# Low words on other engines, and a planner's constants chosen anew

## The chip, the core and the metric

The kernel runs on one core of one Trainium2 chip. A core has TensorE (matrix products, in the profile PE, with its weight loads as PEld), VectorE (DVE), ScalarE (ACT), GpSimd (POOL) and SyncE (SP), which here only issues transfers. Each engine works off its own instructions in order; semaphores tie the engines together. SBUF is the working memory, PSUM takes TensorE's results in banks. The metric is the time of one execution in device microseconds, the median of several runs.

## The reference

Causal attention by blocks of 64, then a feed-forward network over all 4608 tokens, in fp32:

```python
scores = scale * np.matmul(q, k.transpose(0, 1, 3, 2))          # 8 batches, 8 heads, 576 x 576, head size 64
scores = np.where(pos[:, None] // 64 >= pos[None, :] // 64, scores, -1e9)
attn = np.exp(scores - scores.max(-1, keepdims=True))
attn = attn / (attn.sum(-1, keepdims=True) + 1e-9)
x = np.matmul(attn, v).transpose(0, 2, 1, 3).reshape(4608, 512)
h = x @ w_in                                                    # 512 x 2048
out = (np.maximum(h, 0) + alpha * np.minimum(h, 0)) @ w_out     # 2048 x 512
```

The two weight matrices arrive as float64 and reach the chip as pairs of 32-bit words, a low and a high one.

## The kernel before

**Attention** goes over 32 pairs of heads (`NPAIR`), four per batch. For a pair, `scores` runs three groups of query blocks (`TOP`, `MID`, `LOW`): small tiled products on TensorE (L721), maxima per row on VectorE (L726), four exchanges of 32 partitions on GpSimd (`swap`, L698), a minimum on VectorE (L729), exponentials on ScalarE (L734) and transposes on VectorE (L738). `factors_of` makes the reciprocal row sums, `values` the tiled products with v (L780) and the scaling on VectorE (L786). The first 256 rows of a batch run one batch ahead of the others (`SKEW`); so the four pairs of batch 0 come first, with `E0` and `E1` in their priorities.

**The network** is done in two halves. The first six of 16 blocks of the hidden width (`FA`) are worked off during attention, chunk by chunk of 256 tokens: `split_x` parts x in a high and a low piece, `ffn1` makes the hidden products (L508), `activate` the leaky step (L519, L521) and the split of its result into gh (L525 or L527) and gl on GpSimd (L530), `ffn2` the second product (L547). The sum of this half goes to memory (`part`). The other ten blocks come after attention: `later_weights` prepares them, two at a time, `factors` prepares x in 512 tokens, `pair1` makes seven products instead of eight (L588) with additions on VectorE (L597, L601), and `ffn2` and `store_out` finish (L547, L876). Every fp32 product is three products of rounded pieces: high by high, high by low, low by high.

**Conversion of weights** (`to_f32`) makes fp32 out of the word pairs for 128 x 512 values: a load into `raw` (SP), the exponent on VectorE (L391) and ScalarE (L394), the high mantissa on VectorE (L396) and ScalarE (L402), the sign (L399, VectorE), then mantissa = low word x 2^-52 + high part (L403, VectorE), and the product of both parts on GpSimd (L406). There are 32 of them: 12 early ones for the first half (`first_weights`, priorities `C0 + C1 * (f + i / 2)`), 16 during attention whose results are put into memory (`weights_ahead`, priority `5 * p + 100`), and four in `later` for the first pair of blocks: two of w_in at priority `SOON`, two of w_out after attention. Buffers of `raw` and `m` are handed out in program order (`IN_ORDER`). `split` then rounds a weight to its high piece on ScalarE (L411) and subtracts for its low piece (L412), in the second half on the engine that `LATER` names.

**The order** of all this is not written by hand. `Plan.op` collects every step with its engine, an estimated cost, what it reads and writes, and a priority (low goes first); `schedule` plays the engines through in time, and always lets the ready step of lowest priority go whose buffers are free. The resulting order is issued as the program. So a constant that changes no instruction can still change the order on every engine. Attention of pair p has priorities about `5 * p`, with offsets for maxima (`PM`), exponentials (`PX`), transposes (`PT`), row sums (`PZ`) and scaling (`PU`), and `VL` for the load of v; FFN products get theirs from `turn`, and what empties their banks has `FP`. `SHIFTS` adds an amount to all steps of a given priority. `NEAR` lets TensorE stay with tiled products when one is ready whose priority is at most that much higher; `c_tiled` charges `SWITCH` for them, and `schedule` takes it off again when two tiled ones follow one another. `RB`, `EB` and `EF` are the numbers of buffers for `raw`, `m` (converted words) and `ef`.

Of the kernel before, what the change touches and what calls it, by code (L numbers as in the profile page):

```python
# [32 lines left out]
FIRST, THEN = (3, 2, 1, 0), (4,)  # L33
SKEW = 1
DUOS, HB, AB, HT, AM, AT, WB = 3, 2, 1, 3, 2, 4, 4
C0, C1 = -6, 4.5
WARM, WARM_END = 10, 3400
TICK, FULL_COLUMNS, SP0 = 3413.33, 3060, 700
LAG = 5.5
VL = 1.0  # L40
E0, E1 = -2, 1.5
NEAR = 8
FP = -1
AHEAD = {(8, 0): 5, (8, 1): 6, (9, 0): 7, (9, 1): 8, (10, 0): 10, (10, 1): 11, (11, 0): 12, (11, 1): 14, (12, 0): 15, (12, 1): 16, (13, 0): 18, (13, 1): 19, (14, 0): 20, (14, 1): 21, (15, 0): 23, (15, 1): 24}
SHIFTS = {}
SOON, XB = 220, 1004.7
FEW = 10
BEGIN = {"SP": SP0, "ACTQ": SP0, "POOLQ": SP0, "PE": WARM_END, "ACT": 2000, "DVE": 1500, "POOL": 1700}
B1 = 20
RB, EB, EF = 2, 3, 6  # L50
LO_A = ("POOL", "POOL")
QA, VA = 3, 1
PB, QB, VB, TB, CB = 5, 3, 3, 2, 6
SWAP = ("POOL", "POOL", "POOL", "POOL")
RCP = ("ACT", "ACT", "ACT", "ACT")
PM, PX, PT, PZ, PU = -8, -4, -1, -1, -2
XO, XF = 2, 1
GH, XH, XC = ("ACT", "ACT", "POOL"), "ACT", 2
LATER = ("POOL", "POOL", "POOL", "POOL", "POOL", "POOL")
GB = 6  # L60
LAT = {"PE": 240, "DVE": 140, "ACT": 137, "POOL": 95}
LONGER = 1.06
# [23 lines left out]
class Plan:  # L86
# [16 lines left out]
    def op(self, engine, cost, fn, r=(), w=(), prio=0.0, claim=(), then=None, ends=()):  # L103

        i = len(self.ops)
        prio += SHIFTS.get(round(prio, 4), 0.0)
        deps = {j for j, o in enumerate(self.ops) if any(b.kind in ends for b in o[4])} if ends else set()
        for k in r:
            if k in self.writer:
                deps.add(self.writer[k])  # L110
        for k in w:
            if k in self.writer:
                deps.add(self.writer[k])
            deps.update(self.readers.get(k, ()))
        for k in r:
            self.readers.setdefault(k, []).append(i)
        for k in w:
            self.writer[k] = i
            self.readers[k] = []
        bufs = dict.fromkeys(k[0] if isinstance(k, tuple) else k for k in (*r, *w, *claim))  # L120
        bufs = [b for b in bufs if isinstance(b, Buf)]
        for b in bufs:
            b.users += 1
            if b.users == 1 and b.kind in IN_ORDER:
                b.after = self.last.get(b.kind)
                self.last[b.kind] = b
        deps.discard(i)
        self.ops.append((engine, cost, fn, deps, bufs, prio, then))
        return i
# [147 lines left out]
    return (93 if sbuf else 51) + n / 1.2  # L277


SWITCH = 420  # L280


def c_pool(n):
# [18 lines left out]

def c_tiled(n, count):

    return Products(max(4 * n / 2.4, 11 * count) + SWITCH, max(4 * n / 1.2, 22 * count) + 2 * SWITCH, 4 * n, True)


@with_exitstack
def attn_ffn(ctx, tc, qT, kT, vT, w_in, w_out, alpha, out):
# [63 lines left out]
    def to_f32(src, prio, after=(), early=None):  # L373
# [12 lines left out]
        def fr():  # L386
# [13 lines left out]
            out=e(), in0=high(), scalar=-2 ** 31, in1=e(), op0=ALU.bitwise_and, op1=ALU.bitwise_or),  # L400
            r=[raw], w=[ea], prio=prio)
        op("ACT", c_act(512, True), lambda: nc.scalar.activation(out=eb(), in_=fr(), func=AF.Copy, scale=2.0 ** -20), w=[eb], prio=prio)  # L402
        op("DVE", Beside(600), lambda: nc.vector.scalar_tensor_tensor(  # L403
            out=mb(), in0=low(), scalar=2.0 ** -52, in1=eb(), op0=ALU.mult, op1=ALU.add),
            r=[raw, eb], w=[mb], prio=prio)
        op("POOL", c_pool(512), lambda: nc.gpsimd.tensor_tensor(out=mb(), in0=mb(), in1=e().bitcast(F32), op=ALU.mult), r=[ea], w=[mb], prio=prio)  # L406
        return mb, mb

# [454 lines left out]

    def second_room():
        rooms("fx", ("w1", 2, [2, 7 * 256], F32R), ("w2", 4, [2, 512], F32R), ("X", 6, [2, 512], F32R),
              ("g", 2, [CHA], F32), ("gh", 2, [CHA], F32R), ("gl", 2, [CHA], F32R))
    op("NONE", 0, end_first, r=[("xd", b, i, pair) for b in range(B) for i in range(2) for pair in range(NP)], ends=("wa", "xh", "xl", "xc", "xo"), prio=0, then=second_room)

    def store_out(acc, t):
# [55 lines left out]
```

## Time and profile before

| | us |
|---|---|
| Median of the runs (3) | 1053.79, from 1052.94 to 1057.25 |
| Profiled execution, its own time | 1054.86 |
| Its span, first to last instruction | 1053.0 |
| TensorE busy | 1002.1 (95%) |
| VectorE, ScalarE, GpSimd busy | 731.2, 594.0, 586.0 |
| Attention's last tiled product ends | 514.0 |
| First product of the second FFN half starts | 570.2 |

A row of busy time by stage has from:to, its length, then for TensorE, its weight loads, VectorE, ScalarE and GpSimd the busy us and in brackets the instructions, then the granted TensorE clock (1 is full), the busy share of the DMA engines, and GB/s. A row of waits says which engine and line was idle for whom: total us, times, longest. A group of instructions has line, engine, operation, output<-inputs and shapes, count, then busy us, mean ns of one, and the idle time before them. A row in order of time begins with start and length.

### The profile page before, as it was taken

The page shows a single profiled execution, that of the slowest core. Times are in us where ns is not written, and L with a number is a line of the kernel's source. Part 1 is how long each engine was busy: PE and PEld are TensorE (multiplying, and loading weights), DVE is VectorE, ACT ScalarE, POOL GpSimd, SP SyncE. Part 2 cuts the span into 40 slices and gives each one's busy share as a digit, 9 for nine tenths or more (in the row PEclk, how much of TensorE's full clock was granted, in tenths as well). Part 3 has the DMA queues.
Part 4 walks back from the last instruction along what each step waited for, and adds up shares of the span by engine and source line. Part 5 has one row for each costly group of instructions (what it writes and reads, how often), then busy time and mean ns, then how long its engine had stood idle before and what let it go on. Part 6 is the DMA issues. An engine that isn't in the chain of part 4 may idle for free.

```text
span 1053.0 us, 32747 instructions
## 1 busy us (share of the span) xinstructions
PE 1002.1 (95%) x12860; PEld 876.3 (83%) x12860; DVE 731.2 (69%) x1654; ACT 594.0 (56%) x2124; POOL 586.0 (56%) x1038
## 2 busy tenths in 40 slices
PE   5477999999999999999999999999999999999998
PEld 4365788888888888888888988989898989898987
DVE  6999899998786888885553675656565656565552
ACT  6967778877585777666555643434343434343431
POOL 5777647575474665656699962535353525252521
PEclk7698999999999999999999999999999999999999
DMA  8565766665756556632424222121212121212021
GB/s 280 165 218 167 221 210 221 199 213 173 225 165 224 194 166 205 204 119 81 154 71 127 75 71 81 41 80 42 81 41 81 41 81 40 82 41 81 2 81 40
DMA packets 78987, 133.73 MB, mean 127 GB/s; under 512 B 11632, under 2 KB 40048, under 8 KB 78832
## 3 DMA queue, kind: packets, MB, share of 16 engines
q1 hardware_dynamic: 78400, 131.36, 38.4%
q8 instruction: 101, 1.65, 0.7%
q14 instruction: 54, 0.44, 0.1%
q10 hardware_dynamic: 432, 0.27, 0.1%
HBM read 99.10 MB, written 32.51 MB: 125 GB/s over the span
## 4 chain that ended last, share of the span: by engine, by line
PE 65%; POOL 3%; ACT 1%; issue 1%; DVE 1%; DVEq 0%; POOLq 0%; ACTq 0%
PE bank L547 30%; PE bank L588 21%; PE bank L508 8%; PE duo L780 3%; PE duo L721 3%; POOL gl L530 1%; POOL X L412 1%; ACT p L734 1%; POOL xl L496 1%; POOL w L412 0%; POOL c L698 0%; DVE c L726 0%; DVE g L521 0%; DVE m L403 0%; POOL gh L525 0%
## 5 line engine op out<-in xcount | busy, mean ns | idle before, releaser
L530 POOL TENSOR_TENSOR gl<-g,gh 128x256 fp32r<-128x256 f32 x288 | 224.1, 782 | 281.3 <-ACT gh L527 251.7
L588 PEld LDWEIGHTS bank<-X,w 128*128 128x128 f32 x1890 | 254.4, 189 | 21.0 <-POOL X L412 1.3
L588 PE MATMUL bank<-X,w 128*128 128x256 f32 x1890 | 260.3, 282 | 1.6 <-POOL w L412 0.9
L734 ACT ACTIVATE p<-duo,c 128x256 f32<-128x256 f32 (+8 forms) x576 | 220.7, 407 | 44.0 <-DVE c L729 29.4
L547 PE MATMUL bank<-w,gh 128*128 128x512 f32 x720 | 225.4, 394 | 0.0
L519 ACT ACTIVATE g<-bank 128x256 f32<-128x256 f32 x288 | 109.1, 386 | 139.5 <-DVE bank L601 86.6
L521 DVE SCALAR_TENSOR_TENSOR g<-g,oal,bank 128x256 f32<-128x256 f32 x288 | 134.1, 473 | 66.8 <-ACT g L519 62.1
L527 ACT CAST gh<-g 128x256 fp32r<-128x256 f32 x252 | 102.4, 408 | 121.2 <-PE bank L547 93.0
L601 DVE TENSOR_TENSOR bank<-bank,g 128x256 f32<-128x256 f32 x180 | 75.4, 428 | 119.4 <-PE bank L588 116.9
L698 POOL TENSOR_SCALAR c<-c 32x4 f32<-32x4 f32 (+3 forms) x400 | 101.8, 254 | 83.1 <-DVE c L726 45.4
L547 PE MATMUL bank<-w,gl 128*128 128x512 f32 x360 | 141.9, 394 | 0.2 <-POOL gl L530 0.2
L547 PE MATMUL bank<-wa,gh 128*128 128x512 f32 x432 | 138.9, 402 | 2.5 <-ACT wa L411 1.2
L547 PEld LDWEIGHTS bank<-w,gh 128*128 128x128 f32 x720 | 121.1, 188 | 13.5
L726 DVE TENSOR_REDUCE c<-duo 128x2 f32<-128x512 f32 (+8 forms) x288 | 122.3, 477 | 13.9 <-PE duo L721 13.5
L508 PE MATMUL bank<-xh,wa 128*128 128x256 f32 x864 | 126.8, 288 | 1.7 <-POOL wa L412 1.5
L734 ACT ACTIVATION_READ_ACCUMULATOR p<-duo,c 128x1 f32 x576 | 126.0, 219 | 0.0
L508 PEld LDWEIGHTS bank<-xh,wa 128*128 128x128 f32 x864 | 113.1, 191 | 11.6 <-issue 5.4
L738 DVE STREAM_TRANSPOSE PTH<-p 128x576 f32<-128x576 f32 (+4 forms) x160 | 98.1, 627 | 8.8 <-ACT p L734 7.9
L721 PE MATMUL duo<-k,q 64*32 64x192 f32 (+4 forms) x2560 | 84.5, 373 | 19.5 <-ACT p L734 10.5
L547 PEld LDWEIGHTS bank<-wa,gh 128*128 128x128 f32 x432 | 77.9, 188 | 22.7 <-issue 3.0
L547 PE MATMUL bank<-wa,gl 128*128 128x512 f32 x216 | 85.5, 396 | 0.6 <-POOL gl L530 0.6
L597 DVE TENSOR_TENSOR g<-bank,g 128x256 f32<-128x256 f32 x135 | 56.1, 420 | 40.9 <-PE bank L588 40.7
(63 smaller groups left out, 1321.3 us busy)
## 6 DMA issues: line engine op xcount, KB each, us to landing
v<-in_v SPq DMA_DIRECT2D x32, 576.0 KB, 4.4
k<-in_k SPq DMA_DIRECT2D x32, 288.0 KB, 5.1
xb<-xd SPq DMA_DIRECT2D x9, 1024.0 KB, 5.4
m<-part SPq DMA_DIRECT2D x36, 256.0 KB, 3.2
out<-m SPq DMA_DIRECT2D x35, 256.0 KB, 2.0
va<-in_v SPq DMA_DIRECT2D x32, 256.0 KB, 3.2
raw<-in_w_in SPq DMA_DIRECT2D x16, 512.0 KB, 5.1
raw<-in_w_out SPq DMA_DIRECT2D x16, 512.0 KB, 4.6
```

The lines of the kernel that those rows point to most:

```text
L508: nc.tensor.matmul(hp()[:, :n], ww()[:, 0, cc * P:(cc + 1) * P], x()[:, cc, :n], start=(i == 0 and cc == 0), stop=(i == 2 and cc == NCC - 1))
L519: op("ACT", c_act(CHA), lambda: nc.scalar.activation(out=g(), in_=hp()[:, ts], func=AF.Relu, scale=-1.0), r=[hp], w=[g], prio=FP)
L521: op("DVE", c_dve(CHA) + 60, lambda: nc.vector.scalar_tensor_tensor(out=g(), in0=g(), scalar=oal[:, f:f + 1], in1=hp()[:, ts], op0=ALU.mul ...
L527: op("ACT", c_act(CHA, True), lambda: nc.scalar.copy(out=gh(), in_=g()), r=[g], w=[gh], prio=FP)
L530: op("POOL", c_pool(CHA) + 60, lambda: nc.gpsimd.tensor_tensor(out=gl(), in0=g(), in1=gh().bitcast(F32), op=ALU.subtract), r=[g, gh], w=[g ...
L547: nc.tensor.matmul(acc(), a()[:, ts], ww(), start=(first and i == 0), stop=(last and i == 2))
L588: nc.tensor.matmul(bank()[:, :CHA], W()[:, i, 256 * at + P * c:256 * at + P * c + P], B()[:, j, CHA * c:CHA * c + CHA], start=(n == 0), st ...
L698: nc.gpsimd.tensor_scalar(out=o, in0=i, scalar1=scale, scalar2=None, op0=ALU.mult)
L721: nc.tensor.matmul(sb()[32 * i:32 * i + 32, h, off[T]:off[T] + w], q()[hs, qs], blocks(k()[hs], T + 1, 32 * (i % 2)), start=True, stop=True)
L726: op("DVE", c_dve(2 * w), lambda t=t, w=w, o=o: nc.vector.tensor_reduce(out=c()[:, 0, 2 * t:2 * t + 2], in_=sb()[:, :, o:o + w], axis=AX.X ...
L734: op("ACT", 237 + w / 1.2, lambda x=2 * t + h, T=T, h=h, w=w, o=o: nc.scalar.activation(out=pb()[:, 2 * o + h * w:2 * o + h * w + w], in_= ...
L738: op("DVE", 85 + 2.08 * w, lambda to=to, a=a, w=w, o=o: nc.vector.transpose(out=to()[:, a:a + 2 * w], in_=pb()[:, 2 * o:2 * o + 2 * w]), r ...
```

## The change

Three edits to instructions:

- In `to_f32`, a conversion whose priority is under `LOW_POOL` = 6 no longer makes its mantissa in one VectorE instruction. ScalarE scales the low word into `m`, and GpSimd adds the high part to it.
- All six entries of `LATER` are VectorE instead of GpSimd.
- `raw` has four buffers for two, `m` four for three; in the last room gh and gl get one more buffer each instead of two.

The rest changes the planner alone: `VL`, `NEAR`, `FP`, `PM`, `PZ`, `SOON`, `XB`, the charges for tiled products, and 34 entries in `SHIFTS`, which was empty.

```diff
+LOW_POOL = 6
-VL = 1.0
+VL = 0
-NEAR = 8
-FP = -1
+NEAR = 12
+FP = 2
-SHIFTS = {}
-SOON, XB = 220, 1004.7
+SHIFTS = {38.0: 3, 36.5: 1, 28.9815: -1, 57.0: 20, 32.3148: 0.5, 169.7222: -3, 181.5741: -0.5, 148.5: -20, 168.2407: 10, 33.0: -1, -9.0: 1, 43.7963: -3, 44.537: 10, 47.0: -10, 105.0: 10, 57.1296: -3, 130.0: 3, 43.0: 20, 215.0: -1, 170.463: -20, 175.2778: -0.5, 50.463: -2, 171.9444: 20, 62.0: 10, 159.3519: -20, 133.0: 5, 154.1667: -3, 18.5: -20, 54.9074: -2, 11.5: 0.5, 36.0: 2, 43.4259: 3, 20.0: 0.5, 71.5741: 3}
+SOON, XB = 100, 1006.7
-RB, EB, EF = 2, 3, 6
+RB, EB, EF = 4, 4, 6
-PM, PX, PT, PZ, PU = -8, -4, -1, -1, -2
+PM, PX, PT, PZ, PU = -7, -4, -1, 0, -2
-LATER = ("POOL", "POOL", "POOL", "POOL", "POOL", "POOL")
+LATER = ("DVE", "DVE", "DVE", "DVE", "DVE", "DVE")
...
-SWITCH = 420
+SWITCH, RUN = 400, 160
...
-    return Products(max(4 * n / 2.4, 11 * count) + SWITCH, max(4 * n / 1.2, 22 * count) + 2 * SWITCH, 4 * n, True)
+    return Products(max(4 * n / 2.4, 11 * count) + SWITCH + RUN, max(4 * n / 1.2, 22 * count) + 2 * (SWITCH + RUN), 4 * n, True)
...
-        op("DVE", Beside(600), lambda: nc.vector.scalar_tensor_tensor(
-            out=mb(), in0=low(), scalar=2.0 ** -52, in1=eb(), op0=ALU.mult, op1=ALU.add),
-            r=[raw, eb], w=[mb], prio=prio)
+        if prio < LOW_POOL:
+            op("ACT", c_act(512, True), lambda: nc.scalar.activation(out=mb(), in_=low(), func=AF.Copy, scale=2.0 ** -52), r=[raw], w=[mb], prio=prio)
+            op("POOL", c_pool(512), lambda: nc.gpsimd.tensor_tensor(out=mb(), in0=mb(), in1=eb(), op=ALU.add), r=[eb], w=[mb], prio=prio)
+        else:
+            op("DVE", Beside(600), lambda: nc.vector.scalar_tensor_tensor(
+                out=mb(), in0=low(), scalar=2.0 ** -52, in1=eb(), op0=ALU.mult, op1=ALU.add),
+                r=[raw, eb], w=[mb], prio=prio)
...
-              ("g", 2, [CHA], F32), ("gh", 2, [CHA], F32R), ("gl", 2, [CHA], F32R))
+              ("g", 2, [CHA], F32), ("gh", 1, [CHA], F32R), ("gl", 1, [CHA], F32R))
```

## The prediction

> **What bounds the kernel now.** I read the page's head first, then the busy time by stage, then the waits of the first 120 us, and then single rows.
>
> ```profile
> span 1053.0 us, 32747 instructions
> PE 1002.1 (95%) x12860; PEld 876.3 (83%) x12860; DVE 731.2 (69%) x1654; ACT 594.0 (56%) x2124; POOL 586.0 (56%) x1038
> ...
> PEclk7698999999999999999999999999999999999999
> ```
>
> TensorE is busy for 1002.1 of 1053.0 us, and no edit takes a product away. So the time can only come out of the 50.9 us in which TensorE is idle, and out of the low clock of the first slices. The same by stage (columns: the five engines, granted clock, DMA share, GB/s):
>
> ```profile
> 0.00:10.00 10.00, 6.20 (x202) 5.04 (x202) 3.08 (x14) 2.80 (x10) 2.02 (x12) 1.00 0.80 236
> 10.00:60.00 50.00, 27.62 (x772) 20.57 (x772) 45.88 (x127) 42.85 (x195) 37.70 (x82) 0.69 0.66 222
> 60.00:120.00 60.00, 47.31 (x1088) 37.22 (x1089) 54.73 (x131) 44.47 (x182) 41.76 (x84) 0.89 0.63 196
> 120.00:500.00 380.00, 374.07 (x7258) 323.93 (x7260) 316.64 (x743) 277.25 (x1168) 230.47 (x545) 1.00 0.58 186
> 500.00:620.00 120.00, 117.37 (x894) 104.25 (x884) 64.86 (x117) 65.44 (x165) 107.65 (x128) 1.00 0.34 107
> 620.00:1000.00 380.00, 380.00 (x2381) 342.29 (x2380) 223.87 (x477) 148.23 (x375) 154.60 (x174) 1.00 0.17 57
> 1000.00:1053.00 53.00, 49.52 (x283) 43.03 (x281) 22.12 (x49) 12.92 (x34) 11.81 (x16) 1.00 0.17 60
> ```
>
> Idle time of TensorE by stage is length less busy: 3.8 us before 10, 22.4 in 10 to 60, 12.7 in 60 to 120, 5.9 in 120 to 500, 2.6 in 500 to 620, none to 1000, and 3.5 at the tail. So 35.1 of the 50.9 us lie between 10 and 120, where VectorE is busy 92% and 91%, ScalarE 86% and 74%, GpSimd 75% and 70%. The waits of the first 120 us (total, times, longest):
>
> ```profile
> POOL c L698 <- DVE c L726: 14.9, 11, 6.8
> ...
> PE duo L780 <- ACT p L734: 10.9, 5, 5.3
> PE duo L721 <- ACT p L734: 10.8, 8, 3.4
> ACT p L734 <- DVE c L729: 10.3, 5, 6.0
> ...
> POOL m L406 <- DVE m L403: 5.1, 4, 1.8
> ...
> PE bank L508 <- POOL wa L412: 1.5, 2, 1.1
> PE duo L721 <- DMA qa<-in_k: 1.5, 2, 1.3
> ...
> PE bank L547 <- ACT wa L411: 1.2, 1, 1.2
> ...
> PE bank L547 <- POOL wa L412: 1.0, 1, 1.0
> ```
>
> TensorE waits 21.7 us for exponentials; those wait for the maxima (VectorE) and their exchange (GpSimd). Another 3.7 us is for converted weights. The first FFN product starts late:
>
> ```profile
> 57.90 1.22 PE L508 MATMUL bank<-xh,wa 128*128 128x256 f32 x8
> ```
>
> Until then there is only attention to run, so every wait of its chain is idle time.
>
> **Part (a): early lows.** Conversions have priorities -6, -3.75, and so on in steps of 2.25; six of the twelve early ones lie under 6. Later ones start at 100. The prices, from the first 120 us (count, busy us, mean ns):
>
> ```profile
> L412 POOL TENSOR_TENSOR wa<-m,wa 128x512 fp32r<-128x512 f32 x12 | 15.7, 1312 | 4.4 <-ACT wa L411 4.0
> L406 POOL TENSOR_TENSOR m<-m,ef 128x512 f32<-128x512 f32 x12 | 15.3, 1274 | 5.7 <-DVE m L403 5.1
> ...
> L403 DVE SCALAR_TENSOR_TENSOR m<-raw,ef 128x512 f32<-128x512 uint32 x12 | 8.3, 695 | 0.2 <-ACT ef L402 0.2
> ...
> L402 ACT ACTIVATE ef<-ef 128x512 f32<-128x512 int32 x12 | 7.6, 633 | 1.5 <-DVE ef L396 1.4
> ```
>
> VectorE loses 6 x 0.695 = 4.2 us. ScalarE gains a scaled copy of 512 integers, like L402: 6 x 0.633 = 3.8 us. GpSimd gains an add of two 512 wide tiles, like L406: 6 x 1.274 = 7.6 us. All six lie in 10 to 60 us before, as L403's starts in the first 60 us show:
>
> ```profile
> L403 DVE SCALAR_TENSOR_TENSOR m<-raw,ef x6: 674/685/693, 15.9 to 56.3; 128x512 f32<-128x512 uint32 x6
> ```
>
> So that stage would hold 41.7 us on VectorE, 46.7 on ScalarE and 45.3 on GpSimd, of 50. The fullest engine goes from 45.9 to 46.7 us: by load alone nothing is won. What speaks for a gain is the order of the chain: it stands 25.2 us behind VectorE's reductions and minima (14.9 + 10.3). Bounds: -4.2 us, if all that VectorE sheds reaches TensorE, and +3.8 us, if all that ScalarE takes on delays exponentials. Both bounds are near; I take **-1 us**, on VectorE's side because the named waits are there.
>
> **Part (b): rings, and constants of the start.** Raw words get four buffers for two, converted words four for three; FP, PM, PZ, VL and 34 shifts reorder what is ready together. None adds an instruction. The rings allow the last six conversions, which stay on VectorE, to be loaded and begun earlier. What is there to win is the 3.7 us of waits for weights, and at most all 35.1 us of idle; to lose, two more raw loads ahead of q, k and v on SP's queue: 512 KB each at the 222 GB/s of that stage is 2.3 us, so +4.6 us, against 1.5 us of such waits now. FP = 2 lets the first two pairs go ahead of the first chunk's split; behind them wait only FFN products that cannot start before 57.9. I take **-3 us**, four fifths of the waits for weights, and nothing of the attention chain, for which no edit names a shorter path.
>
> **Part (c): tiled runs.** The charges (SWITCH 400 plus RUN 160, for 420) and NEAR 12 for 8 alter no instruction; they make the planner put tiled products (scores, values) together. Of such runs there are 55, counted in the order of time; the first and the last:
>
> ```profile
> 4.74 2.57 PE L721 MATMUL duo<-qa 64*32 64x128 f32 x128 [1.34 <-DMA qa<-in_k]
> ...
> 511.51 0.40 PE L547 MATMUL bank<-wa,gl 128*128 128x512 f32 x1
> 511.84 2.18 PE L780 MATMUL duo<-PTH,v 64*64 64x160 f32 x72
> 513.95 0.74 PE L547 MATMUL bank<-wa,gh 128*128 128x512 f32 x2
> 514.52 0.40 PE L547 MATMUL bank<-wa,gl 128*128 128x512 f32 x1
> 514.76 0.62 PE L547 MATMUL bank<-wa,gh 128*128 128x512 f32 x2
> ```
>
> Each row gives start, length and count. In this stream a 512 wide product starts 0.24 us after the one before (514.52 to 514.76). From 511.51 into the run it is 0.33, and the two behind the run take 0.57 instead of 0.48 (513.95 to 514.52). So entering and leaving cost some 0.09 us each. Five to ten runs fewer give 0.9 to 1.8 us, as many more lose that; by the wider NEAR I take **-0.5 us**, three runs fewer.
>
> **Part (d): later lows on VectorE, SOON, gh and gl, XB.** The lows and their nearest rows on VectorE, over the whole span:
>
> ```profile
> L412 POOL TENSOR_TENSOR w<-m,w 128x512 fp32r<-128x512 f32 x20 | 26.3, 1319 | 0.1
> L412 DVE TENSOR_TENSOR X<-xt,X 128x512 fp32r<-128x512 f32 x18 | 26.2, 1456 | 9.7 <-ACT X L411 9.7
> ...
> L412 POOL TENSOR_TENSOR w<-ws,w 128x512 fp32r<-128x512 f32 (+1 forms) x10 | 10.1, 1013 | 0.0
> ...
> L412 DVE TENSOR_TENSOR X<-xb,X 128x512 fp32r<-128x512 f32 x9 | 6.7, 744 | 0.0
> ```
>
> GpSimd sheds 36.4 us. VectorE takes 25 subtractions of 512 and 5 of 256 (counted as halves: 27.5) at 0.744 to 1.456 us, so 20.5 to 40.0 us. Nearly all falls into 500 to 620: GpSimd goes from 107.7 to 71 us, VectorE from 64.9 to 85 or 105 of 120. SOON lets two conversions of w_in go earlier within attention (two raw loads, eight VectorE, four ScalarE and two GpSimd instructions up to the product). Since raw buffers are handed out in program order they stay behind the 16 conversions ahead of them; running products cover them (374.1 of 380 us), and uncovered they would be four VectorE steps each, 2 x 4 x 0.695 = 5.6 us. TensorE's waits in 120 to 620:
>
> ```profile
> PE bank L588 <- POOL w L412: 0.9, 1, 0.9
> PE bank L547 <- POOL gl L530: 0.7, 2, 0.6
> PE bank L588 <- POOL X L412: 0.7, 2, 0.4
> ```
>
> That is all there is to win, 2.3 us; the products of the first FFN half cover the rest, and if that cover were gone, the uncovered excess would be what VectorE takes, 20.5 to 40 us. I take **-0.8 us**, a third, because VectorE now holds lows before the additions that free the banks. One buffer less of gh and gl costs nothing: from 620 to 1000 TensorE has no idle to show that it runs short; the same rows cover XB.
>
> The Trainium skill, SBUF — State Buffer, section "SBUF: two separate sides", says that a VectorE instruction with two SBUF inputs and a GpSimd instruction that reads SBUF exclude each other for a whole instruction. The 1456 beside the 744 ns agrees with it. By this rule alone each later low is priced at its blocked mean, 40 us, and (d) is a loss, the fourth rival below.
>
> **Part (e): the clock.** In 60 to 120 the granted clock is 0.89. If low means half, 60 x 0.11 x 2 = 13 us ran at half rate; at the busy share of 79% that lost 5.2 us. If 3 of the 12.7 us of idle go, I count that share of it: **-1.2 us** (bounds 0 and -5.2).
>
> **Sum.** -1 - 3 - 0.5 - 0.8 - 1.2 = -6.5 us. The profiled execution took 1054.86 us, 1.86 around its span, so it would become 1048.4. It is 1.07 above the median of the runs shown, 1053.79; against that median the forecast is 1047.3 us.
>
> **Rivals.**
>
> *Nothing to measure.* The load row of (a), 46.7 for 45.9 us, holds; the start stays bound by three full engines, idle merely changes place, and (c) to (e) give 1 us. Time 1052.8. For it: TensorE is at 99% from 120 us on whatever is reordered. Against it: 35.1 us of idle lie together in the stage that most constants touch.
>
> *Large gain.* The first chunk's x is done earlier, so the FFN fills the chain's waits before 57.9. Half of the 22.4 us goes, with (b) to (e): 1053.8 - 11.2 - 5.5 = 1037.1. For it: the first weights are split long before 57.9:
>
> ```profile
> 19.33 1.27 POOL L412 TENSOR_TENSOR wa<-m,wa 128x512 fp32r<-128x512 f32 x1
> ```
>
> Against it: the constants that set this pace (E0, E1, C0, C1, LAG) stay.
>
> *Slower: ScalarE and GpSimd become the early bound.* In each of six conversions a 0.63 us copy stands ahead of exponentials and a second 1.27 us add ahead of the four small exchanges that the next minimum waits for: 6 x 1.907 - 4.2 = +7.2 us, and what (b) gives is lost behind it: 1061. It decides when the idle of 10 to 60 passes 26 us and the first FFN product starts after 60. For it: both engines at over 90% of that stage. Against it: GpSimd idles 5.1 us there for L403 itself.
>
> *The later lows lock out GpSimd.* At the blocked price of 1.456 us VectorE holds 105 of 120 us in 500 to 620, each low stands ahead of the additions that free banks, and GpSimd's gl waits behind it. If the first FFN half is used up by then, the 19.5 us between the two prices reach TensorE: 1053.8 + 19.5 - 5.7 for (a), (b), (c) and (e) = 1067.6. It decides when L588 or L547 wait more than 5 us there. For it: the two prices of one instruction. Against it: VectorE is empty for 55 of these 120 us.
>
> **How the numbers follow.** A change within 0.5% (5.3 us) counts as no change. Forecast 0.45, large gain 0.08, nothing to measure 0.35, early bound 0.08, lock 0.04. Faster is 0.45 + 0.08 = 0.53, same 0.35, slower 0.12. The likeliest case by itself spans 1043 to 1049; the range 1040 to 1057 takes in the no-change case and leaves out most of the large gain and the slower ones.
>
> **What would show it.** (a) L403 runs 26 times, not 32, and VectorE's busy time in 10 to 60 falls towards 42 us while ScalarE's rises over 45. (b) TensorE's waits for wa in the first 120 us fall under 1 us, and idle in 10 to 120 is near 31. (c) Fewer than 50 tiled runs. (d) GpSimd under 80 us in 500 to 620, and no new wait of L588 or L547 for VectorE. (e) Clock over 0.91 in 60 to 120. The forecast is wrong if the idle of 10 to 120 stays over 34 us, or if any comes up after 620.

## The result, and the profile after

The changed kernel takes **1061.31 us** (median of 6 runs, 1059.93 to 1063.12) against 1053.77 us of the kernel before on the same chip (median of 6, 1052.28 to 1057.25). The ratio is 1.007, 95% interval 1.0056 to 1.0085: slower by 0.7%, where 1047.3 was forecast with a range of 1040 to 1057. The profiled execution took 1059.93 us. Lines of the changed kernel carry numbers 1 higher up to L403 and 5 higher from L408 on: L408 is the old L403, L417 the old L412, L513, L552 and L593 the old L508, L547 and L588, L726 and L785 the tiled products L721 and L780. L405 and L406 are the two new instructions, and the old L406 is L411. In e1 the lines behind the edit are 4 higher.

The head of the page of the kernel after:

```profile
span 1058.1 us, 32734 instructions
PE 1005.4 (95%) x12860; PEld 877.2 (83%) x12860; DVE 750.1 (71%) x1678; ACT 599.8 (57%) x2130; POOL 560.7 (53%) x1014
```

The span grew by 5.1 us, TensorE's idle time only from 50.9 to 52.7. The other 3.3 us are busy time of the same 12860 products, which ran or overlapped more slowly. So idle alone doesn't tell where the time went. By stage (columns as before):

```profile
10.00:60.00 50.00, 24.20 (x640) 16.25 (x648) 46.32 (x118) 43.38 (x187) 38.11 (x78) 0.82 0.63 218
60.00:120.00 60.00, 51.29 (x1124) 41.38 (x1116) 56.37 (x125) 45.91 (x186) 46.53 (x89) 0.86 0.56 178
120.00:500.00 380.00, 373.98 (x7329) 323.61 (x7315) 313.04 (x751) 278.47 (x1176) 229.76 (x547) 1.00 0.60 190
500.00:620.00 120.00, 114.94 (x901) 100.87 (x901) 87.51 (x147) 65.92 (x164) 82.02 (x99) 1.00 0.34 106
```

TensorE idles 25.8 us in 10 to 60 (22.4 before), 8.7 in 60 to 120 (12.7), 6.0 in 120 to 500 (5.9), 5.1 in 500 to 620 (2.6). The sum of 10 to 120 is 34.5 against 35.1: the stage at which most of the change was aimed is where it was.

To count slow products too, I worked out a **loss** from each trace: the time passed, less what the products begun by then take at full rate. The full rate of each shape is its mean spacing in the trace of the kernel before, after 130 us, long pauses left out. Where these are cut off moves the levels: with spacings of 0.25 us and more left out, every figure of a stage comes out up to 1.6 us higher, and differences between runs move by 0.5 at most. In us:

```
                 to 120   120-500   500-620   end
before             63.0      21.5       3.9   87.8
after              64.7      21.3       7.8   92.9
```

So the 5.1 us are +1.7 before 120 us, -0.2 in 120 to 500, +3.9 in 500 to 620, and -0.3 later. The medians lie 7.5 us apart, 2.4 more than this pair of profiles. The experiments below contain kernels whose order on all four engines is that of one of these two up to some 515 us or further than the stage in question, so each stage has several profiles (before, e2, e9, e10, e11, e13, e17, in the second stage without e9, e10 and e17; after, e4, e8, e14, in the second without e8; the mean in brackets):

```
                 to 120                                        120-500
order of before  63.0 61.7 61.6 62.6 63.0 64.4 62.1 (62.6)     21.5 20.3 19.9 21.4 (20.8)
order of after   64.7 65.2 63.8 64.6                (64.6)     21.3 24.3 21.4      (22.3)
```

With these means the difference is +2.0, +1.5 and +3.9, 7.4 us in all, about the distance of the medians. One profile of a stage can be off by 2 us or so; the +3.9 is the surest of the three, and the +1.5 hangs on the 24.3 of one profile. It has two parts, too: by the same means the order of after loses 3.5 us more between 120 and 215 us and 2.0 less between 215 and 500, where its three profiles lie within 0.2 us of each other and the four of before within 1.4. So part of the new order is better, and a stage's sum hides it.

**The early stage.** Waits of the first 120 us, after:

```profile
ACT p L739 <- DVE c L734: 16.5, 10, 6.0
POOL c L703 <- DVE c L731: 14.6, 8, 6.9
PE duo L785 <- ACT p L739: 13.6, 5, 4.6
PE duo L726 <- ACT p L739: 9.9, 5, 4.9
...
DVE c L734 <- POOL c L703: 3.2, 8, 0.7
PE duo L726 <- DMA qa<-in_k: 3.1, 3, 1.4
...
PE bank L552 <- POOL wa L417: 1.2, 1, 1.2
...
PE bank L552 <- ACT wa L416: 0.7, 1, 0.7
PE bank L513 <- ACT wa L416: 0.6, 1, 0.6
...
PE bank L513 <- POOL wa L417: 0.3, 1, 0.3
```

It is the same chain as before, maxima, exchange, minimum, exponentials: TensorE waits 23.5 us for exponentials (21.7 before). The load of q and k costs 3.1 us for 1.5. Weights are waited for 2.8 us (3.7 before); but nothing was won by it. The early lows did leave VectorE, and the moved instructions cost what was assumed:

```profile
L408 DVE SCALAR_TENSOR_TENSOR m<-raw,ef x26: 627/682/1776, 65.0 to 535.5; 128x512 f32<-128x512 uint32 x26
```

```profile
L405 ACT ACTIVATE m<-raw x6: 650/668/728, 15.6 to 54.5; 128x512 f32<-128x512 uint32 x6
```

```profile
L406 POOL TENSOR_TENSOR m<-m,ef x6: 1262/1266/1280, 16.4 to 57.3; 128x512 f32<-128x512 f32 x6
```

Yet VectorE's busy time in 10 to 60 didn't fall by 4.1 us, it rose from 45.88 to 46.32. Groups of VectorE between 10 and 58 us, first before, then after (last number ahead of the bar: count; behind it busy us, mean ns):

```profile
L396 DVE TENSOR_SCALAR ef<-raw 128x512 int32<-128x512 int32 x6 | 4.0, 669 | 0.0
L399 DVE SCALAR_TENSOR_TENSOR ef<-raw,ef 128x512 int32<-128x512 int32 x6 | 4.0, 667 | 0.0
...
L746 DVE SCALAR_TENSOR_TENSOR z<-z 128x8 f32<-128x8 f32 x4 | 1.1, 272 | 0.7 <-POOL z L698 0.7
...
L729 DVE SCALAR_TENSOR_TENSOR c<-c 128x10 f32<-128x10 f32 x3 | 0.5, 171 | 0.9 <-POOL c L698 0.8
```

```profile
L400 DVE SCALAR_TENSOR_TENSOR ef<-raw,ef 128x512 int32<-128x512 int32 x6 | 5.4, 899 | 0.2 <-ACT ef L395 0.2
...
L397 DVE TENSOR_SCALAR ef<-raw 128x512 int32<-128x512 int32 x6 | 4.6, 764 | 0.0
L751 DVE SCALAR_TENSOR_TENSOR z<-z 128x8 f32<-128x8 f32 x4 | 2.7, 668 | 0.6 <-POOL z L703 0.6
...
L734 DVE SCALAR_TENSOR_TENSOR c<-c 128x10 f32<-128x10 f32 x2 | 1.4, 678 | 0.0
```

The same instructions take longer: 6 x 0.232 + 6 x 0.095 + 4 x 0.396 + 2 x 0.507 = 4.6 us, which uses up the 6 x 0.684 = 4.1 us shed. An 8 or 10 wide operation that lasts 0.67 instead of 0.17 to 0.27 us isn't computing all that time, it is held up. The means come from eight long instances, of 0.87 to 1.76 us. In order of time, each of them has a GpSimd instruction of 512 elements running at its start, and ends with that one or at most one free duration later. In four cases it is one of the six new adds (L406), in the other four it is L411 or L417, which the kernel before has as well. So the new adds account for part of the stretching alone, the new places of old instructions for the rest. The Trainium skill, SBUF — State Buffer, section "SBUF: two separate sides", names what fits this: VectorE with two SBUF inputs, or in a mode that uses two ports, and GpSimd reading SBUF shut each other out for a whole instruction. The trace agrees for L400, L734 and L751, which have two such inputs; L397 has one, and no view tells whether it runs in such a mode.

**500 to 620.** TensorE's waits from 500 to 625 us, after (those of before stand in the prediction):

```profile
PE bank L552 <- ACT gh L532: 1.4, 2, 0.8
PE bank L593 <- DVE X L417: 1.3, 1, 1.3
PE bank L513 <- POOL xl L501: 0.9, 1, 0.9
PE bank L593 <- DVE g L526: 0.5, 1, 0.5
PE bank L552 <- POOL gl L535: 0.4, 2, 0.3
PE bank L593 <- POOL X L417: 0.2, 1, 0.2
```

The lows on VectorE cost 1.05 us, about midway between the two prices of the prediction, and GpSimd's own work there got slower. VectorE after, then GpSimd before and after:

```profile
L417 DVE TENSOR_TENSOR w<-m,w 128x512 fp32r<-128x512 f32 x20 | 20.9, 1050 | 4.3 <-ACT w L416 4.1
```

```profile
L530 POOL TENSOR_TENSOR gl<-g,gh 128x256 fp32r<-128x256 f32 x41 | 32.4, 805 | 3.5 <-ACT gh L527 2.5 <-POOL c L698 0.7
```

```profile
L535 POOL TENSOR_TENSOR gl<-g,gh 128x256 fp32r<-128x256 f32 x41 | 35.2, 866 | 23.7 <-ACT gh L532 13.6 <-issue 4.0 <-PE bank L593 2.3
```

### The profile page after: what moved, and what is told of

It is laid out like the page before. It is cut to its first block, busy times and chain, and to the rows that moved or that the text cites. A ratio compares the mean times of both kernels' runs of the same rounds, so it can differ in the third digit from the quotient of the medians.

```text
span 1058.1 us, 32734 instructions
## 1 busy us (share of the span) xinstructions
PE 1005.4 (95%) x12860; PEld 877.2 (83%) x12860; DVE 750.1 (71%) x1678; ACT 599.8 (57%) x2130; POOL 560.7 (53%) x1014
## 3 DMA queue, kind: packets, MB, share of 16 engines
q8 instruction: 101, 1.65, 0.7%
## 4 chain that ended last, share of the span: by engine, by line
PE 79%; POOL 8%; DVE 5%; ACT 4%; issue 3%; DMA 1%; SPq 0%; POOLq 0%; DVEq 0%; ACTq 0%
PE bank L552 34%; PE bank L593 20%; PE bank L513 12%; PE duo L726 6%; PE duo L785 6%; POOL c L703 2%; ACT p L739 2%; POOL gl L535 1%; POOL m L411 1%; POOL xl L501 1%; POOL z L703 1%; DVE c L731 1%; POOL wa L417 1%; DVE PTH L743 1%; DMA qa<-in_q 1%
## 5 line engine op out<-in xcount | busy, mean ns | idle before, releaser
L593 PEld LDWEIGHTS bank<-X,w 128*128 128x128 f32 x1890 | 255.2, 189 | 21.9 <-DVE X L417 1.7
L593 PE MATMUL bank<-X,w 128*128 128x256 f32 x1890 | 261.3, 282 | 2.1 <-DVE X L417 1.3
L552 PE MATMUL bank<-w,gh 128*128 128x512 f32 x720 | 225.3, 394 | 0.6 <-ACT gh L532 0.6
L532 ACT CAST gh<-g 128x256 fp32r<-128x256 f32 x252 | 102.7, 408 | 138.1 <-PE bank L552 117.4
L526 DVE SCALAR_TENSOR_TENSOR g<-g,oal,bank 128x256 f32<-128x256 f32 x288 | 132.7, 472 | 39.7 <-ACT g L524 35.1
L703 POOL TENSOR_SCALAR c<-c 32x4 f32<-32x4 f32 (+3 forms) x400 | 100.0, 250 | 88.8 <-DVE c L731 63.5
L552 PE MATMUL bank<-wa,gh 128*128 128x512 f32 x432 | 140.1, 405 | 3.5 <-POOL wa L417 1.2
L552 PE MATMUL bank<-w,gl 128*128 128x512 f32 x360 | 141.8, 394 | 0.1
L552 PEld LDWEIGHTS bank<-w,gh 128*128 128x128 f32 x720 | 120.7, 188 | 13.7 <-ACT gh L532 0.8
L513 PE MATMUL bank<-xh,wa 128*128 128x256 f32 x864 | 125.9, 287 | 1.8 <-ACT o L658 0.9
L513 PEld LDWEIGHTS bank<-xh,wa 128*128 128x128 f32 x864 | 112.7, 190 | 11.7 <-issue 3.9
L743 DVE STREAM_TRANSPOSE PTH<-p 128x384 f32<-128x384 f32 (+4 forms) x160 | 99.0, 628 | 17.8 <-ACT p L739 16.3
L726 PE MATMUL duo<-k,q 64*32 64x192 f32 (+4 forms) x2560 | 84.6, 376 | 15.6 <-ACT p L739 10.2
L552 PEld LDWEIGHTS bank<-wa,gh 128*128 128x128 f32 x432 | 78.1, 190 | 24.4 <-issue 2.3
L552 PE MATMUL bank<-wa,gl 128*128 128x512 f32 x216 | 86.2, 399 | 1.0 <-POOL gl L535 0.9
```

Of the source, the lines that this page charges most:

```text
L513: nc.tensor.matmul(hp()[:, :n], ww()[:, 0, cc * P:(cc + 1) * P], x()[:, cc, :n], start=(i == 0 and cc == 0), stop=(i == 2 and cc == NCC - 1))
L526: op("DVE", c_dve(CHA) + 60, lambda: nc.vector.scalar_tensor_tensor(out=g(), in0=g(), scalar=oal[:, f:f + 1], in1=hp()[:, ts], op0=ALU.mul ...
L532: op("ACT", c_act(CHA, True), lambda: nc.scalar.copy(out=gh(), in_=g()), r=[g], w=[gh], prio=FP)
L552: nc.tensor.matmul(acc(), a()[:, ts], ww(), start=(first and i == 0), stop=(last and i == 2))
L593: nc.tensor.matmul(bank()[:, :CHA], W()[:, i, 256 * at + P * c:256 * at + P * c + P], B()[:, j, CHA * c:CHA * c + CHA], start=(n == 0), st ...
L703: nc.gpsimd.tensor_scalar(out=o, in0=i, scalar1=scale, scalar2=None, op0=ALU.mult)
```

## The experiments

The question of all of them: does an edit cost the time by what its instructions do, or by the new order that the planner draws once anything in it is altered? So three kinds were made: an edit with the order of the other instructions **kept**, an edit alone with the order **planned anew**, and changes **without meaning** that only make the planner draw again. "Loss" is that defined above; all figures together, in us (ratio to the kernel before on the same chip, with its 95% interval):

```
                                     median   ratio  [interval]         to 120  120-500  500-620
order kept
e1  before, early lows moved        1063.22  1.0090 [1.0073,1.0107]      69.6    22.5      3.0
e2  before, later lows moved        1054.23  0.9998 [0.9988,1.0008]      61.7    20.3      3.8
e3  after, early lows back          1063.45  1.0085 [1.0070,1.0100]      65.2    23.6      8.3
e4  after, later lows back          1074.98  1.0201 [1.0184,1.0218]      65.2    24.3     21.2
e17 e9's order, later lows moved    1050.77  0.9953 [0.9933,0.9973]      62.1    20.4      3.4
one edit alone, planned
e5  early lows                      1061.25  1.0071 [1.0049,1.0093]      70.5    23.3      2.9
e6  rings                           1061.78  1.0083 [1.0064,1.0101]      65.0    24.8      3.2
e7  charges, NEAR                   1063.16  1.0093 [1.0075,1.0111]      70.2    22.6      2.6
e11 later lows                      1058.15  1.0031 [1.0021,1.0042]      63.0    19.9      7.7
e13 later lows, GpSimd's cost       1057.53  1.0040 [1.0024,1.0056]      64.4    21.4      7.5
after without one edit, planned
e8  without shifts                  1064.85  1.0118 [1.0093,1.0143]      63.8    25.9      8.2
e12 without early lows              1064.19  1.0089 [1.0073,1.0106]      65.2    24.7      8.5
e14 without later lows              1059.53  1.0056 [1.0040,1.0073]      64.6    21.4      7.5
without meaning, planned
e9  before, 1 ns                    1049.07  0.9945 [0.9926,0.9965]      61.6    16.4      3.2
e10 before, cost factor 1.062       1056.39  1.0020 [1.0008,1.0033]      62.6    20.4      4.5
e15 after, 1 ns                     1071.38  1.0168 [1.0147,1.0189]      65.6    30.2      8.7
e16 early lows, 1 ns                1064.81  1.0101 [1.0072,1.0130]      70.5    23.1      2.7
e18 charges, 1 ns                   1067.03  1.0111 [1.0088,1.0134]      70.2    29.1      2.4
```

To read the table one has to know from where on an order differs. Compared instruction by instruction on the four compute engines, e9 has the order of before up to 215 us, e10 up to 122, e11 and e13 up to 515; e14 has that of after up to 517, e8 up to 149, e15 up to 78. e16 has that of e5 up to 361, e18 that of e7 up to 372. The other planned ones differ from before and after within the first 36 us.

### Moves with the order kept

**e1**, in the kernel before; the step keeps its place in the plan and issues other instructions:

```diff
-        op("DVE", Beside(600), lambda: nc.vector.scalar_tensor_tensor(...), r=[raw, eb], w=[mb], prio=prio)
+        def mantissa():
+            if prio < 6:
+                nc.scalar.activation(out=mb(), in_=low(), func=AF.Copy, scale=2.0 ** -52)
+                nc.gpsimd.tensor_tensor(out=mb(), in0=mb(), in1=eb(), op=ALU.add)
+            else:
+                nc.vector.scalar_tensor_tensor(out=mb(), in0=low(), scalar=2.0 ** -52, in1=eb(), op0=ALU.mult, op1=ALU.add)
+        op("DVE", Beside(600), mantissa, r=[raw, eb], w=[mb], prio=prio)
```

> The kernel before, its order kept on every engine: only the six early lows are made on ScalarE and GpSimd at the place where VectorE's instruction stood. Theory L (the extra GpSimd adds lock VectorE's two-input instructions and take GpSimd from the exchanges, whatever the order): 2 to 5 us slower than before, VectorE's busy time in 10 to 60 us not lower than 45 in spite of six instructions fewer. Theory O (the order from the new constants is the cause): within 1.5 us of before. Theory F (the forecast's part a): 1 us faster.

It cost 0.9%. Its stage 10 to 60, and three waits of the first 120 us (L405 and L406 are the copy and the add here, too):

```profile
10.00:60.00 50.00, 25.11 (x656) 16.75 (x656) 36.68 (x105) 41.88 (x184) 36.52 (x78) 0.71 0.59 197
```

```profile
DVE c L733 <- POOL c L702: 15.2, 14, 2.6
ACT p L738 <- DVE c L733: 14.0, 8, 6.2
...
POOL m L406 <- ACT m L405: 4.2, 4, 1.5
```

and the first of them in the kernel before:

```profile
DVE c L729 <- POOL c L698: 4.5, 10, 0.9
```

VectorE is busy for 9 us less, 4 of them for the six instructions, the rest because attention's work comes later (105 instructions for 127). Its minima wait 15.2 us for the exchanges for 4.5, because 1.27 us adds stand ahead of them on GpSimd, which itself waits 4.2 us for the copies that these adds need. In this order the move costs 8.5 us (1063.22 less 1054.69), more than theory L's 2 to 5, and VectorE is far under the 45 us that theory L named. What happens is what the prediction's third rival said of the exchanges; by 120 us the loss is 69.6, far outside the 61.6 to 64.4 of the seven profiles of that order.

**e2** and, later, **e17** emit the later lows on VectorE at the places planned for GpSimd (e17 with `SWITCH = 421`, e9's order); **e4** does the reverse in the order of after:

```diff
+EMIT = "DVE"        # e4, in the kernel after: "POOL"
-    def split(src, hi, lo, n, r, hk, lk, claim, on, prio):
+    def split(src, hi, lo, n, r, hk, lk, claim, on, prio, emit=None):
-        ... (nc.gpsimd if on == "POOL" else nc.vector).tensor_tensor(
+        ... (nc.gpsimd if (emit or on) == "POOL" else nc.vector).tensor_tensor(
```

> The kernel before, its order kept: only the later lows are made on VectorE, at the place where they stood on GpSimd. Theory S (second half: VectorE holds these subtractions ahead of what frees banks and makes x's pieces): 2 to 4 us slower, with TensorE waiting for VectorE in 500 to 620 us. Theory O: within 1.5 us. Theory F: 0.8 us faster.

> The order drawn with the charge of 421 ns for 420, which came out at 1049.07 us, kept, with the later lows issued on VectorE in their places. If, as in the order of the kernel before, the move costs nothing where the order is kept: 1047 to 1051, loss of 500 to 620 us near 3. If VectorE's lows cost 3.9 us in any order: 1052 to 1054.

> The kernel after, with its order; only the later lows go back to GpSimd at the places that they have on VectorE. Theory S: 2 to 4 us faster than after, 1057 to 1059. Theory O: as after, or slower, since this order was planned with a free GpSimd: 1060 to 1064.

In e2 and e17 the move costs nothing that can be measured; the intervals of e17 and e9 overlap. Back on GpSimd in the order drawn for VectorE (e4) they cost 13.7 us more, nearly all in 500 to 620: an order planned for one engine doesn't suit the other, and e4 therefore doesn't price the edit.

**e3** puts the early lows back on VectorE at the places of GpSimd's adds in the order of after:

```diff
-            op("ACT", ..., lambda: nc.scalar.activation(out=mb(), in_=low(), func=AF.Copy, scale=2.0 ** -52), r=[raw], w=[mb], prio=prio)
-            op("POOL", ..., lambda: nc.gpsimd.tensor_tensor(out=mb(), in0=mb(), in1=eb(), op=ALU.add), r=[eb], w=[mb], prio=prio)
+            op("ACT", ..., lambda: None, r=[raw], w=[mb], prio=prio)
+            op("POOL", ..., lambda: nc.vector.scalar_tensor_tensor(out=mb(), in0=low(), scalar=2.0 ** -52, in1=eb(), op0=ALU.mult, op1=ALU.add), r=[raw, eb], w=[mb], prio=prio)
```

> The kernel after, with its order of products; only the six early lows go back to one VectorE instruction at the place of the GpSimd add. Theory L: 2 to 5 us faster than after, so 1056 to 1059, and the first FFN product up to 5 us earlier than 66.7. Theory O: as after, 1060 to 1062.

It isn't faster than after. Its first FFN product does come earlier, at 63.5 us, and that wins nothing. In the order drawn for them, the moved early lows aren't what holds the kernel back; but as in e4, an edit undone in an order made for it shows no more than that.

### One edit alone, planned anew

Each is one of the diff's parts put into the kernel before: **e5** `LOW_POOL` and its branch, **e6** the rings, **e7** the charges and `NEAR`, **e11** `LATER`; **e13** is e11 with the old price:

```diff
-RB, EB, EF = 2, 3, 6                                    # e6
+RB, EB, EF = 4, 4, 6
-... ("gh", 2, [CHA], F32R), ("gl", 2, [CHA], F32R))
+... ("gh", 1, [CHA], F32R), ("gl", 1, [CHA], F32R))
-NEAR = 8                                                # e7, with c_tiled as in the change
+NEAR = 12
-SWITCH = 420
+SWITCH, RUN = 400, 160
-        op(on, c_pool(n) + 60 if on == "POOL" else Beside(c_dve(n)), ...
+        op(on, c_pool(n) + 60 if on == "POOL" or prio >= 1000 else Beside(c_dve(n)), ...      # e13
```

> The kernel before with the early lows moved and nothing else, planned anew for it. If the move costs by itself even where the planner can make room (theory L): 1058 to 1064 us, as with the order kept. If only a bad place cost there (theory P, the plan decides): 1053 to 1057.

> The kernel before with four raw and four converted buffers and one gh and gl less, planned anew. If larger rings let conversions run ahead of attention on VectorE and take it from the first chunk (theory R): 3 to 6 us slower and the first FFN product after 60 us. If they do nothing or help (forecast's part b): 1050 to 1055.

> The kernel before with SWITCH 400, RUN 160 and NEAR 12 alone, planned anew. If the charges carry the loss (theory C): 1057 to 1063. If they are worth what the forecast said: 1052 to 1055.

> The kernel before with the later lows on VectorE, planned anew; its order is that of before up to some 470 us. Theory B with a loss only where the order differs: 1053 to 1056, since the early order is kept. If the later lows cost by themselves once planned: 1056 to 1060, with the loss between 500 and 620 us.

> The kernel before with the later lows on VectorE, planned anew, but with the planner charging GpSimd's cost for them, so that it paces them as it did before. Theory P (the 3.9 us that the kernel after loses between 500 and 620 us come from pacing VectorE's lows by a price that the lock with GpSimd breaks): the loss of that stage stays near the 3.9 us of the kernel before, and the time is 1052 to 1056. Theory Q (VectorE's lows cost it wherever they are planned): the loss is near 7.8 us, as in the run that has this edit alone, and the time is 1057 to 1060.

All five are slower than before, by 0.3 to 0.9%. e5 loses it by 120 us, like e1 (70.5 and 69.6 for 62.6); its two early stages have 21.1 and 15.8 us of idle:

```profile
10.00:60.00 50.00, 28.94 (x712) 20.57 (x715) 41.94 (x114) 43.20 (x185) 38.63 (x78) 0.62 0.60 203
60.00:120.00 60.00, 44.20 (x974) 33.69 (x961) 51.19 (x119) 42.38 (x173) 43.24 (x84) 0.75 0.56 178
```

Here VectorE does fall to the 42 us that the prediction named, and it helps nothing. Nor does an early start of the FFN: its first product begins at 49.7 us in e5 and at 50.5 in e7 (57.9 before), and these two lose the most by 120 us. e7 ends up at 70.2 with charges alone, which act through the order and nothing else; e6 loses 2.4 us early and 4 in 120 to 500.

e11 and e13 are the cleanest pair: all that they lose comes after 515 us, 7.7 and 7.5 us of loss in 500 to 620 for 3.9, and 3.7 and 3.8 us of time. Pacing by a wrong price isn't the reason, since e13 has the old one: theory P falls. With e2 the reading is that the later lows on VectorE are harmless where they are issued at GpSimd's places, and cost some 4 us where the planner places them, in both of the two plans.

### The whole change less one edit

```diff
-SHIFTS = {38.0: 3, 36.5: 1, ...}       # e8
+SHIFTS = {}
-LOW_POOL = 6                           # e12
+LOW_POOL = -99
-LATER = ("DVE", ...)                   # e14
+LATER = ("POOL", ...)
```

> The kernel after with no shifts, planned anew. If the 34 shifts fit the planner's own clock and not the chip (theory S): faster than after, 1053 to 1059. If they help on the chip: 1062 to 1070.

> The kernel after with the early lows on VectorE, planned anew with all its other constants. If the early low is what costs (theory L): 1053 to 1057. Theory B: 1059 to 1066, not better than after.

> The kernel after with the later lows back on GpSimd, planned anew. If the later lows carry the 3.9 us of 500 to 620, the loss of that stage falls from 7.8 to about 3 us and the time is 1056 to 1059, unless the new order's stretch up to 500 us comes out worse by as much. If the stage's loss has another cause, it stays at 7 to 8 us and the time at 1061 or more.

Without the shifts it is slower still, by 3.5 us (medians); that is less than a single nanosecond does to this kernel below. Taking out the early lows doesn't help, though alone they cost 8.5 us. e14 contradicts the story that the later lows cause after's loss in 500 to 620: they are on GpSimd again (106.79 us), and that stage is as bad as in after, 7.5 us of loss for 7.8. (Its time, 1059.53, lies between those of the two theories.)

```profile
500.00:620.00 120.00, 114.97 (x904) 101.65 (x904) 66.85 (x117) 66.04 (x164) 106.79 (x126) 1.00 0.33 99
```

```profile
PE bank L513 <- POOL xl L501: 1.5, 1, 1.5
PE bank L593 <- POOL X L417: 0.8, 2, 0.6
```

Up to 517 us its order is that of after, so nothing else hides this. There are two ways into this loss: the later lows by themselves (e11, e13), and something else in the change, which is there without them. Of the rest, rings and charges alone leave the stage at 3.2 and 2.6 us, the early lows at 2.9. `SOON`, `FP`, the other priorities and the shifts remain; they weren't run singly. The shifts aren't needed for it, nor are the early lows: without them the stage loses 8.2 (e8) and 8.5 (e12). Which it is stays open.

### Changes without meaning

```diff
-SWITCH = 420            # e9; e16 the same with e5's edit
+SWITCH = 421
-LONGER = 1.06           # e10
+LONGER = 1.062
-SWITCH, RUN = 400, 160  # e15 in the kernel after, e18 with e7's edit
+SWITCH, RUN = 401, 160
```

> The kernel before with SWITCH 421 for 420: no instruction and no intent changes, but the planner's clock shifts by 1 ns per tiled step and other orders come out. If the order before is one of many alike (theory A): 1051 to 1056 us. If it is a rare good one that any new plan gives up (theory B): 1058 to 1064, as with the four edits planned anew.

> The kernel before with LONGER 1.062 for 1.06, a second edit without intent. Theory A: 1051 to 1056 us. Theory B: 1058 to 1064.

> The kernel after with one charge a single ns higher (401 for 400), planned anew: an edit without meaning of its own. Theory E (the loss belongs to the edits): 1059 to 1064, loss by 120 us at least 64, loss of 500 to 620 near 8. Theory D (the loss is the draw of the order): like the two such edits of the kernel before, which came out at 1049.1 and 1056.4, it can fall by 5 us or more, to 1056 or below.

> The early lows alone moved, planned anew, with one charge a single ns higher (421 for 420). Theory E (the moved lows themselves cost the early stage): the loss by 120 us stays near the 69.6 to 70.5 us of the two runs with the moved lows, 7 us above the kernel before, and the time is 1058 to 1065. Theory D (the draw): the loss by 120 us falls to 61 to 65, as in the kernel before and its two edits of that kind, and the time to 1050 to 1057.

> The searched charges alone, planned anew, with one charge a single ns higher (401 for 400). Theory E (the charges themselves are worse): 1060 to 1066, loss by 120 us near 70 again. Theory D (the draw): loss by 120 us 61 to 66 and 1050 to 1058.

A charge of 421 ns for 420, which describes nothing on the chip better or worse, made the kernel before 5.4 us faster (e9). Its order begins to differ at 215 us; between there and 500 the two profiles of e9's order (e9, e17) lose some 3 us less than the four of before's order. 401 for 400 made the kernel after 10.1 us slower (e15). e9 beats both kernels:

```profile
span 1045.7 us, 32746 instructions
...
120.00:500.00 380.00, 378.21 (x7386) 328.14 (x7385) 317.81 (x753) 280.53 (x1184) 234.41 (x554) 1.00 0.59 186
```

while e15 loses most of its 10 us (a loss of 30.2 for 21.3) in the stage that the prediction held for covered:

```profile
120.00:500.00 380.00, 369.79 (x7263) 314.46 (x7246) 307.99 (x734) 270.47 (x1146) 228.20 (x535) 1.00 0.59 188
```

e16 and e18 don't settle theory E against theory D. Their early losses are those of e5 and e7 (70.5 and 70.2), as E expects, but the nanosecond left the order of these stages as it was up to 361 and 372 us, so nothing was drawn again there. What they show is that such an early loss repeats when the order does, and that e18 loses another 6.5 us in 120 to 500, some 4 of them after 350 us, where its order departs from e7's.

So, sorted by how sure it is. **Shown:** an order carries -5 to +10 us, most of it in 120 to 500, that no edit explains (e9, e15); the early lows cost 8.5 us where the rest of the order is kept (e1); the later lows cost nothing with the order kept (e2, e17) and 4 us planned (e11, e13). **Not shown:** which part of the change brings after its +3.9 us in 500 to 620, where the loss is there with the later lows and without them; and which edit brings +2.0 us by 120 and +1.5 in 120 to 500. Early lows alone or charges alone make the early stage worse (70.5 and 70.2) than the whole change does (64.6), and taking out one edit at a time never restores the kernel before. These 3.5 us may well be a draw: the two orders of the whole change, after and e15, are 10.1 us apart.

## Why the prediction was wrong

- **(a) Early lows, -1 us: wrong in sign where it could be measured.** The counts were right (26 times L408, 0.67 and 1.27 us for the new instructions), VectorE at 42 and ScalarE above 45 us were not (46.3 and 43.4). The step weighed loads per engine and took VectorE's side "because the named waits are there". But the chain runs through GpSimd's exchanges too, and adds of 1.27 us ahead of them are paid by the minima that wait (15.2 us for 4.5): +8.5 us with the order kept (e1), and +8.5 in one plan with this edit alone (e5, 1061.25 less 1052.75). In after the stretched VectorE instructions take back the 4.1 us shed; there, though, the minima wait only 3.2 us for the exchanges, and taking the edit out helps nothing (e12), so it isn't shown to cause after's own early loss.
- **(b) Rings and start constants, -3 us: not there.** The waits for weights shrank from 3.7 to 2.8 us, not under 1, and idle of 10 to 120 is 34.5 for 35.1, over the bound of 34 that was to refute the forecast. The weights don't come earlier, for all the buffers: ten of the twelve lows (L417) start later than before, the first at 20.4 for 19.3, the last at 108.5 for 106.2. And attention's chain sets the time: the fourth scaling, which the first chunk needs, ends at 56.9 for 49.9, and the first FFN product starts at 66.7 instead of 57.9. What a planner does with more buffers was priced at the waits they can remove, not at the new order, which with the rings alone cost 9.0 us in one plan (e6, 1061.78 less 1052.75).

```profile
66.71 0.74 PE L513 MATMUL bank<-xh,wa 128*128 128x256 f32 x4
```

- **(c) Tiled runs, -0.5 us: nothing.** There are 55 as before, where three fewer were forecast, and 120 to 500 is level in this pair (21.3 for 21.5). The number of runs doesn't even tell the time: e9, the fastest, has 60.
- **(d) Later lows, SOON, -0.8 us: wrong in sign, +3.9 us of loss.** GpSimd went to 82 and not 71 us, and TensorE got new waits, for L532, L417 and L501, each near 1 us. The step held that products in flight cover all but 2.3 us of this stage; that cover failed, with idle of 5.1 us for 2.6. VectorE's lows took 1.05 us on average, between the free price and the blocked one. Yet neither theory of the step holds: with the order kept the move is free, and without it the loss stays.
- **(e) Clock, -1.2 us: not there.** The grant in 60 to 120 is 0.86 for 0.89. But profiles of one order range from 0.86 to 0.91 (before's) and from 0.86 to 0.97 (after's) there, so a single pair could have shown the forecast 0.91 or not. The clock of 10 to 60 can't be compared at all: the first clock record lies at 8.4 us in the trace of before and at 31.9 in that of after, and the time ahead of it counts as full.
- **The rivals.** "ScalarE and GpSimd become the early bound" gave 1061, the measured number, and its second condition came true (66.7, over 60). Its first didn't (idle 25.8, under 26), and its time was to be lost early, where after loses 2.0 us. So the number is luck. It describes e1, by the place of the loss and by the waits, and not after; e5 loses as much early, but with the first FFN product at 49.7. "Nothing to measure" had the early idle right, which changed place and not size, and missed 500 to 620. "Lock" was to show by waits of over 5 us for L593 or L552; they are 3.8 in all.
- **What was missing** altogether is a term for the draw: the sum had a line for each edit and none for 32 thousand instructions being put into another order. Worth -5 to +10 us, it is as large as the whole sum of -6.5.

## What to carry to other kernels

Where a planner orders the program, measure first how far a meaningless change of its constants moves the time; a forecast or a search that looks for less than that spread must try several orders for each edit. Compare the orders first: two kernels often share theirs up to some point, and only what lies behind it can be put down to the edit. Look up a pause that waits for nothing among the instruction packets of the trace. And a step moved off the fullest engine is no gain if it lands ahead of a short link of the chain on another.

## What the runs showed of the hardware

**TensorE waits for its own instructions.** In 120 to 500 us TensorE's idle time in the kernel before is mostly ahead of tiled products, and waits for nothing that the waits name:

```profile
PE duo L721 <- issue: 4.1, 6, 1.1
PE duo L780 <- issue: 1.1, 1, 1.1
```

What ends these pauses stands among the DMA packets. One queue carries instructions in 101 packets of 16 KB (packets, MB, share of 16 engines):

```profile
q8 instruction: 101, 1.65, 0.7%
```

1.65 MB for TensorE's 25720 products and weight loads are 64 bytes each, so the size fits its stream, and a packet holds some 250 of them. In the 20 profiles TensorE has 119 such pauses in this stage, of 0.15 to 3.5 us, and every one ends 1.20 to 1.64 us after a packet of q8 has landed; of the 85 pauses with a named wait, 8 do. A packet takes 1.0 us (median), 2.6 at most, while a run of tiled products goes through instructions fast: the one at 511.84 in the prediction takes 72 products with as many loads in 2.2 us. That fits the place of the pauses.

Their sum is 1.0 us in e9, 5.7 in e15 and 8.5 in e18 (2.5 in e7), and over all 20 profiles it goes with the loss of that stage (correlation 0.75). So part of what an order is worth there lies in these pauses. They also differ between profiles of one order (5.2 in before, 3.1 in e2; e9 has 1.0 and e17 2.7). What makes a packet come late in one execution and not in another stays open.

**A pause can be followed by half clock.** In e17 one of 1.9 us, ending at 133.1, is followed by 3.4 us at half the clock, where e9 in the same order runs through (its packet of instructions landed at 129.2 us, that of e17 at 131.7, while the products of e9 run 0.4 us ahead of those of e17):

```profile
132.00:133.00 1.00, 0.00 (x0) 0.00 (x0) 0.85 (x3) 0.94 (x5) 0.33 (x2) 1.00 0.72 267
133.00:134.00 1.00, 0.93 (x39) 0.93 (x38) 0.96 (x2) 0.20 (x2) 0.00 (x0) 1.00 0.07 28
134.00:135.00 1.00, 1.00 (x15) 0.96 (x8) 0.00 (x0) 0.00 (x0) 0.00 (x0) 0.58 0.13 40
135.00:136.00 1.00, 1.00 (x7) 1.00 (x6) 0.00 (x0) 0.00 (x0) 0.00 (x0) 0.50 0.69 152
136.00:137.00 1.00, 1.00 (x7) 1.00 (x7) 0.36 (x1) 0.78 (x4) 0.00 (x0) 0.50 0.96 369
137.00:138.00 1.00, 1.00 (x8) 1.00 (x7) 1.00 (x3) 0.97 (x5) 0.00 (x0) 0.71 0.19 74
```

That makes 1.9 + 3.4 / 2 = 3.6 us, nearly all of the 3.8 us by which their losses differ between 120 and 150 us. The Trainium skill, TensorE: Matmul & The Clock Gate, "Part 1: The HAM clock gate", speaks of an idle window of about 3.4 us ahead of the low clock; here 1.9 us of idle came ahead of it.
